# 128 bytes before the weight tiles, and one joint back step per head pair, in a sparse-attention, mixing and MLP kernel

## The chip, the cores and the metric

The kernel runs on one core of one Trainium2 chip. The metric is the device time of one execution in microseconds (us), as the median of several runs. The core has five engines with their own instruction streams: PE (TensorE, matrix products; its weight loads are listed apart as PEld), DVE (VectorE), ACT (ScalarE), POOL (GpSimd) and SP (SyncE, which here only issues DMAs). They wait for one another by semaphores. Matrix products read two operands from SBUF, a stationary one, which a weight load puts into the array, and a moving one, which streams through; they write to PSUM, which has eight banks.

## The reference

```python
def _attn_ref(q, k, v, tau):                 # 4 batches, 8 heads, 576 rows, 64 columns
    scores = 1/sqrt(64) * q @ k.T
    thresh = max(scores, -1) - tau
    attn = exp(where(scores >= thresh, scores, -1e9) - max)
    attn = attn / (sum(attn) + 1e-09)
    return attn @ v
def _moe_ref(x, U, V, w_ch1, w_ch2):         # x: 4 x 576 x 512
    u = x + (x.T @ U @ V).T                  # mixing over the rows, rank 32
    return u + relu(u @ w_ch1) @ w_ch2       # 512 -> 2048 -> 512
def _moe2_ref(x, w_val, conv_w, w_out):
    gate = sigmoid(causal 5-tap convolution of x over the rows, by column)
    return (gate * (x @ w_val)) @ w_out
```

The MLP weights arrive as 64-bit floats and are turned into float32 on the chip. Products of the MLP are made of float32 values split into a high and a low part (`float32r`), with three products for each (high-high, high-low, low-high).

## The kernel before

**Attention.** Two heads form a pair; there are 16 pairs. The 576 rows of a pair's two heads make nine blocks of 128 rows: block 0 holds the last 64 rows of both heads, blocks 1 to 8 alternate between the heads. The main loop runs over *slots* `s`, nine to a pair, one block in each. In slot `s` the engines do this, in the order of the code: `soft_max` of block `s` on DVE (`ns`, L409); then four lists of postponed work, `late[0]` to `late[3]`, filled by `later(slot, list, ...)` and sorted within a list by `LATE_ORDER`; the exponential of block `s` on ACT (`e`, L423) after list 1; the mask and row sum of block `s-1` on DVE (L434) after list 2. Then PE's events of the slot follow, sorted by `ORDER`: the scores of the next block (`s`, L395), the transposes of block `s-2` (`xm`, L451, and for even blocks `xk`, L468), and what the `put` calls assign to the slot.

Counted from a pair's first slot `s0`: the products with V (`pv`, tiles `o`) stand in slots 8 (groups 0 and 1) and 12 (group 2), and their copies to SBUF (`os`, ACT) one slot later. `back` transposes `os` into a PSUM tile `b`, and its results are multiplied by the reciprocal row sums `r` and put into `ring`: for groups 1 and 2 by DVE (L521, 256 columns each), for group 0 by ACT (three small instructions, L534 and L536 twice). `back` of groups 0 and 1 stands in slot 10, of group 2 in slot 14. The row mixing reads `ring`: `mix_t` (`t`, L551) in slot 15, `mix_u` and `mix_ut` in slot 18. A pair's slots 9 to 18 are the next pair's slots 0 to 9. **Below, slots are those of the pair whose scores run**, so `back` stands in slots 1 and 5, `mix_t` in slot 6, `mix_u` and `mix_ut` in slot 0. In slots 0, 1 and 2 `prep_T` transposes q, k and the tails of the pair after it (`tm`, L332 and L335); ACT (L310, L312) and DVE (L316, L320) split them one slot later.

All of `xm`, `xk`, `o`, `b`, `t`, `u`, `ut` and `tm` are PSUM tiles of one pool, `x_ps`, with four banks. A new tile takes the bank that was let go first, so PE waits in the program for the last reader of an older tile. In slot 2 the tile `tm` of the tails (L335) takes the bank of `b`, which both ACT and DVE read; `xm` in slot 3 takes the bank of slot 2's `xm`, or that of `tm` of k.

Between the lists a staged converter (`work.tick`) puts weight conversion steps into the streams of ACT, DVE and POOL (L100 to L128, L167, L169).

**The MLP.** `dense` runs over four chunks `c` of 512 hidden columns and five blocks `n` of rows (four of 512, one of 256). `passes` (L771) makes 48 products per block: `a` with `w1[c % 2]` (stationary) and `us` (moving), `c` with `w2[c % 2]` and `h`. At the end `v` uses `w1[0]` and `us`, and `p` (L917) has a part of `g` as stationary and `w2[0]` as moving operand. Chunks 0 and 2 read `w1_0` and `w2_0`, chunks 1 and 3 `w1_1` and `w2_1`.

Pools lay tiles one behind the other, from the low end of a partition or, with `side="right"`, from the high end. First byte in a partition, before the change:

| tile | placed from | byte | remainder by 512 |
|---|---|---|---|
| `ring` | low | 54112 | 352 |
| `w1_0` | low, behind `ring` | 59232 | 352 |
| `w2_0` | low | 75616 | 352 |
| `w1_1` (pool `big`) | low | 145504 | 96 |
| `w2_1` | high | 163808 | 480 |
| `us`, and the second `us` at the MLP's start | high | 212960, 163808 | 480 |
| `h`, later `g` (two buffers) | high | 180192, 196576 | 480 |

Within these tiles every 128 x 128 weight block and every moving block begins a multiple of 512 bytes further on.

Of the kernel before, what the change touches and what calls it, by code (L numbers as in the profile page):

```python
# [21 lines left out]
F32 = mybir.dt.float32  # L22
# [3 lines left out]
ACTF = mybir.ActivationFunctionType  # L26
ALU = mybir.AluOpType
# [9 lines left out]
def attention_moe_kernel(  # L37
# [15 lines left out]
    nc = tc.nc  # L53
    B, H, S, D = q.shape
# [12 lines left out]
    TL = S - SM  # L67
# [11 lines left out]
    const = ctx.enter_context(tc.tile_pool(name="const", bufs=1))  # L79
    idn = const.tile([128, 128], F32, name="idn")  # L80
# [3 lines left out]
    qscale = const.tile([128, 1], F32, name="qscale")  # L84
    cw = const.tile([128, KC, KD], F32, name="cw")
    u = const.tile([128, KD, T], F32, name="u")
    ring = const.tile([128, 1280], F32, name="ring")
    w1_0 = const.tile([128, 2, KD, FC], F32R, name="w1_0")
    w2_0 = const.tile([128, 2, KD, FC], F32R, name="w2_0")
    wst_p = ctx.enter_context(tc.tile_pool(name="wst", bufs=2))  # L90
# [83 lines left out]
    class Staged:  # L174
# [20 lines left out]
    AT = {  # L195
        "pv": (8, 12), "t": 15, "ut": 18, "u": 18, "Tq": 0, "Tk": 1, "Tt": 2, "stA": 4, "bd": 4, "stB": 5,
        "lq": 1, "lv": 5,
    }
# [24 lines left out]
    def attention(dense_front, dense_mid, dense_back):  # L223
        setup = low.enter_context(tc.tile_pool(name="setup", bufs=1))
        sm_p = low.enter_context(tc.tile_pool(name="sm", bufs=4))
# [23 lines left out]
        st8 = [dict() for _ in range(NP)]  # L249

        def xtile(name):
            return x_ps.tile([128, 512], F32, tag="x", name=name)
# [47 lines left out]
        def later(s, k, fn, name=""):  # L300
            late[k].setdefault(s, []).append((LATE_ORDER.get(name, 0), fn))
# [126 lines left out]
        def row(p, i):  # L428
            return st8[p]["e", i][:, 1 - i % 2 if i else 0, :]

        def soft_mask(p, i):
            d = st8[p]
            e = row(p, i)
            nc.vector.scalar_tensor_tensor(  # L434
                out=e, in0=d.pop(("ns", i)), scalar=d.pop(("th", i))[:, 0:1], in1=e, op0=ALU.is_le, op1=ALU.mult,
                accum_out=d["sum"][:, i:i + 1],
            )
            if i in (4, 8):
                n = slice(0, 5) if i == 4 else slice(5, 9)
                t = d["sum"][:, n]  # L440
                nc.vector.tensor_scalar(out=t, in0=t, scalar1=1e-9, scalar2=None, op0=ALU.add)
                nc.vector.reciprocal(out=d["r"][:, n], in_=t)


        def trans_main(s, p, i):
# [41 lines left out]
        def pv(s, p, *gs):  # L487
            d = st8[p]
            ops = []
            for g in gs:  # L490
                n = 256 if g else TL
                pt = d.pop(("pt", g))
                o = xtile("o")
                nc.tensor.matmul(  # L494
                    o[:, 0:n], vk[p % 2].rearrange("p h d -> p (h d)"), d.pop(("pk", g)), start=True, stop=False
                )
                for j in range(4):
                    for hh in range(2):
                        rhs = pt[:, hh, j, :] if g else pt[:, j, hh * TL:(hh + 1) * TL]
                        ops.append((o[hh * D:(hh + 1) * D, 0:n], vt[p % 2][:, hh, j, :], rhs, j == 3))  # L500
                d["os", g] = os = o_p.tile([128, n], F32, tag=f"os{n}", name="os")
                later(s + 1, 0, lambda os=os, o=o, n=n: nc.scalar.activation(
                    out=os, in_=o[:, 0:n], func=ACTF.Copy), "o")
            for o, lhs, rhs, stop in ops:
                nc.tensor.matmul(o, lhs, rhs, start=False, stop=stop)  # L505


        def back(s, p, *gs):
            x = xtile("b")
            for g in gs:  # L510
                back_group(s, p, g, x)

        def back_group(s, p, g, x):
            d = st8[p]
            os, r = d.pop(("os", g)), d["r"]
            if g:
                for m in range(2):
                    nc.tensor.transpose(x[:, m * 128:(m + 1) * 128], os[:, m * 128:(m + 1) * 128], idn)

                def dve():  # L520
                    nc.vector.tensor_tensor(  # L521
                        out=x_of(p)[:, 2 * g - 2:2 * g, :].rearrange("p t (h d) -> p (t h) d", h=2),
                        in0=x[:, 0:256].rearrange("p (t d) -> p t d", t=4),
                        in1=r[:, 4 * g - 3:4 * g + 1].unsqueeze(2).to_broadcast([128, 4, D]), op=ALU.mult,
                    )

                later(s + 1, 2, dve, "n")
            else:
                x = x[0:TL, 256:384]
                nc.tensor.transpose(x, os[:, 0:TL], idn)  # L530
                rb = sm_p.tile([TL, 1], F32, tag="rb", name="rb")

                def act():
                    nc.scalar.activation(out=rb, in_=r[TL:128, 0:1], func=ACTF.Copy)  # L534
                    for hh, sc in ((0, r[0:TL, 0:1]), (1, rb)):
                        nc.scalar.activation(  # L536
                            out=x_of(p)[0:TL, 4, hh * D:(hh + 1) * D], in_=x[:, hh * D:(hh + 1) * D],
                            func=ACTF.Copy, scale=sc,
                        )

                later(s + 1, 1, act, "nt")

        def x_of(p):
            return ring[:, p % 2 * 640:(p % 2 + 1) * 640].rearrange("p (t d) -> p t d", t=5)
# [39 lines left out]
        for m in range(2):  # L584
# [7 lines left out]
            out=rv[0][:, 0:8 * R].rearrange("p (t r) -> p t r", t=4),  # L592
            in_=moe_U[0:SM, :].rearrange("(t p) r -> p t r", p=128),
# [3 lines left out]
        def load_V(a, o, c, n):  # L597
# [5 lines left out]
            out=qscale, in0=tau_sb, scalar1=0.0, scalar2=float(D) ** -0.5, op0=ALU.is_ge, op1=ALU.mult  # L603
# [39 lines left out]
        def put(s, what, *a):  # L643
            slots[s].append((what, a))

        for p in range(NP):
            s0 = 9 * p
            for i in range(9):
                put(s0 + i + 2, trans_main, p, i)
                if i % 2 == 0:  # L650
                    put(s0 + i + 2, trans_tail, p, i)
            put(s0 + AT["pv"][0], pv, p, 0, 1)
            put(s0 + AT["pv"][0] + 2, back, p, 0, 1)
            put(s0 + AT["pv"][1], pv, p, 2)
            put(s0 + AT["pv"][1] + 2, back, p, 2)
            if p + 1 < NP:
                s1 = s0
                put(s1 + AT["Tq"], prep_T, p + 1, "q")
                put(s1 + AT["Tk"], prep_T, p + 1, "k")
                put(s1 + AT["Tt"], prep_T, p + 1, "tail")  # L660
                put(s1 + AT["stA"], stacks, p + 1, 0)
                put(s1 + AT["bd"], tails, p + 1)
                put(s1 + AT["stB"], stacks, p + 1, 1)
            put(s0 + AT["t"], mix_t, p)
            put(s0 + AT["ut"] - (p == NP - 1), mix_ut, p)
            put(s0 + AT["u"] - (p == NP - 1), mix_u, p)
# [7 lines left out]
        for s in range(NS):  # L674
            p, i = divmod(s, 9)
# [12 lines left out]
            for m in (0, 1, 2, 3):  # L688
                for _, fn in sorted(late[m].pop(s, []), key=lambda x: x[0]):
                    fn()  # L690
                if m == 1 and live:
                    soft_exp(p, i)
                if m == 2 and 1 <= s <= 9 * NP:
                    soft_mask(*divmod(s - 1, 9))
                wtick(m)
# [269 lines left out]
    with tc.manual_schedule():  # L965
        attention(dense_front(), dense_mid, dense_back)
        dense()
# [30 lines left out]
```

## Time and profile before

| | us |
|---|---|
| median of 3 runs (867.21, 868.8, 869.0) | 868.8 |
| the profiled execution, its own time | 867.01 |
| its span in the trace | 865.1 |
| PE busy | 834.6 (96%) |
| DVE busy | 615.9 (71%) |
| ACT busy | 439.9 (51%) |
| POOL busy | 233.4 (27%) |
| `a` and `c` products of the MLP (L771) | 205.6 and 203.0 |

Attention fills the span up to about 345 us, the MLP the rest. The granted clock of TensorE is 1.00 of 2.4 GHz in both stages and 0.87 only between 20 and 60 us. A row of the timeline has the start, the time from there to the end of the last instruction of the group, the engine, line and operation, the tiles (out<-in), the shape and the count; in brackets stands the idle time before it and what ended it. The ends of matrix products are modelled, their starts are recorded.

### The profile page before, as it was taken

Reading aid. Unit: us, or ns where it says so; the run is one execution under the profiler, and the core shown is the slowest. Engines: PE = TensorE matmul, PEld = TensorE weight load, DVE = VectorE, ACT = ScalarE, POOL = GpSimd, SP = SyncE. Lnnn points to the kernel's source line nnn. Section 1 sums busy time; section 2 is a strip of 40 time slices with the busy share of each in tenths; the row PEclk is TensorE's granted clock in tenths of the full one; section 3 lists DMA queues with packets and bytes.
Section 4 is the critical chain, followed back from the end, with each engine's and each line's share of the span. In section 5 each row is a group of like instructions: output and inputs, shape, how many; then the busy total and the mean of one; then the engine's idle time right before and its main releaser. Section 6 shows DMA issues by size and latency. Waiting matters only on the chain.

```text
span 865.1 us, 14250 instructions
## 1 busy us (share of the span) xinstructions
PE 834.6 (96%) x5084; PEld 692.8 (80%) x5084; DVE 615.9 (71%) x1341; ACT 439.9 (51%) x890; POOL 233.4 (27%) x342
## 2 busy tenths in 40 slices
PE   8899999999999999899999999999999999999998
PEld 7687787788787887678888888888888888878886
DVE  5589889889989987436784685357753588988850
ACT  4487888888887887422333333133321334344532
POOL 6645422533322422001331243003420133200000
PEclk9799999999999999999999999999999999999999
DMA  5676755666676651001220122002110111001111
GB/s 129 147 151 124 172 125 125 153 154 137 151 168 135 132 113 44 0 1 49 73 74 25 48 74 74 1 1 84 62 50 1 41 57 49 1 1 49 49 49 74
DMA packets 63423, 68.07 MB, mean 79 GB/s; under 512 B 43333, under 2 KB 46549, under 8 KB 63354
## 3 DMA queue, kind: packets, MB, share of 16 engines
q1 hardware_dynamic: 61786, 64.07, 30.3%
q0 software_dynamic: 1424, 3.10, 1.3%
q8 instruction: 41, 0.67, 0.3%
q14 instruction: 28, 0.23, 0.1%
q10 hardware_dynamic: 144, 0.00, 0.0%
HBM read 35.89 MB, written 4.72 MB: 47 GB/s over the span
## 4 chain that ended last, share of the span: by engine, by line
PE 77%; DVE 9%; ACT 8%; issue 2%; SPq 1%; POOL 1%; DMA 1%; ACTq 0%; DVEq 0%; POOLq 0%
PE a L771 23%; PE c L771 20%; PE o L505 7%; PE s L395 6%; PE p L917 6%; PE xm L451 5%; PE v L771 5%; DVE u L855 3%; ACT e L423 2%; PE t L551 2%; PE o L494 2%; ACT pt L460 2%; DVE ns L409 1%; DVE e L434 1%; ACT qk L310 1%
## 5 line engine op out<-in xcount | busy, mean ns | idle before, releaser
L771 PE MATMUL a<-us,w 128*128 128x512 f32 (+1 forms) x960 | 205.6, 373 | 0.0
L771 PE MATMUL c<-h,w 128*128 128x512 f32 (+1 forms) x960 | 203.0, 370 | 1.3 <-ACT u L573 1.3
L771 PEld LDWEIGHTS a<-us,w 128*128 128x128 f32 x960 | 167.6, 188 | 33.9 <-issue 0.4
L771 PEld LDWEIGHTS c<-h,w 128*128 128x128 f32 x960 | 167.4, 188 | 33.7 <-ACT u L573 1.7
L779 ACT ACTIVATE h<-a 128x512 fp32r<-128x512 f32 (+1 forms) x80 | 44.2, 554 | 202.9 <-PE a L771 202.9
L780 DVE SCALAR_TENSOR_TENSOR h<-a,h 128x512 fp32r<-128x512 f32 (+1 forms) x80 | 51.0, 637 | 112.3 <-ACT h L779 112.2
L423 ACT ACTIVATE e<-ns,nm 128x576 f32<-128x576 f32 x144 | 111.5, 774 | 36.1 <-DVE ns L409 32.7
L128 POOL TENSOR_TENSOR wf<-wf,wt 128x512 f32<-128x512 f32 (+2 forms) x43 | 57.1, 1329 | 262.7 <-DVE wt L123 262.7
L424 POOL TENSOR_TENSOR th<-nm,tau_eff 128x1 f32<-128x1 f32 x144 | 72.8, 506 | 195.5 <-DVE ns L409 193.9
L434 DVE SCALAR_TENSOR_TENSOR e<-ns,th,e 128x576 f32<-128x576 f32 x144 | 119.8, 832 | 5.9 <-POOL th L424 5.5
L409 DVE TENSOR_SCALAR_CACHE_REDUCE ns<-s 128x576 f32<-128x576 f32 x144 | 107.8, 748 | 19.8 <-PE s L395 19.3
L451 PE MATMUL xm<-idn,e 128*128 128x128 f32 x576 | 88.5, 277 | 9.4 <-DVE e L434 5.1
L395 PE MATMUL s<-st 128*128 128x288 f32 x480 | 94.0, 317 | 1.3 <-DVE ns L409 1.1
L460 ACT ACTIVATE pt<-xm 128x512 f32<-128x512 f32 x144 | 84.5, 587 | 2.7 <-PE xm L451 0.6
L451 PEld LDWEIGHTS xm<-idn,e 128*128 128x128 f32 x576 | 69.1, 141 | 15.3 <-ACT pt L460 8.7
L395 PEld LDWEIGHTS s<-st 128*128 128x128 f32 x480 | 68.7, 191 | 13.5 <-DVE ns L409 6.6
L505 PE MATMUL o<-pt,vt 128*64 128x256 f32 (+1 forms) x768 | 70.9, 335 | 0.0
L505 PEld LDWEIGHTS o<-pt,vt 128*64 128x64 f32 x768 | 42.1, 140 | 25.2 <-issue 10.8
L169 POOL TENSOR_TENSOR w<-wf,w 128x512 fp32r<-128x512 f32 x36 | 54.2, 1518 | 10.3 <-ACT w L167 10.3
L832 DVE TENSOR_TENSOR y<-c,y 128x64 f32<-128x64 f32 (+4 forms) x96 | 39.9, 449 | 22.0 <-PE c L771 22.0
L855 DVE SCALAR_TENSOR_TENSOR u<-y,cw,u 128x576 f32<-128x576 f32 x64 | 55.0, 872 | 0.6
L756 DVE TENSOR_TENSOR us<-u,us 128x1024 fp32r<-128x1024 f32 (+1 forms) x40 | 46.8, 1211 | 9.2 <-ACT us L755 9.1
(108 smaller groups left out, 1043.8 us busy)
## 6 DMA issues: line engine op xcount, KB each, us to landing
raw<-in_moe_w_ch_dram SPq DMA_DIRECT2D x32, 512.0 KB, 4.1
st<-qk SPq DMA_DIRECT2D x30, 256.0 KB, 4.1
st<-qk SPq DMA_DIRECT2D x15, 432.0 KB, 4.0
st<-qk SPq DMA_DIRECT2D x45, 144.0 KB, 4.5
out_dram<-ring SPq DMA_DIRECT2D x18, 256.0 KB, 2.0
st<-qk SPq DMA_DIRECT2D x15, 288.0 KB, 4.9
qn<-in_q_dram SPq DMA_DIRECT2D x28, 128.0 KB, 3.8
kn<-in_k_dram SPq DMA_DIRECT2D x28, 128.0 KB, 3.6
```

Source lines behind the costliest of these rows:

```text
L128: nc.gpsimd.tensor_tensor(out=dst, in0=dst, in1=tf, op=ALU.add)
L169: lo_eng.tensor_tensor(out=lo, in0=w, in1=f(hi), op=ALU.subtract)
L395: nc.tensor.matmul(s[:, n, 0:HS], lhs, rhs[:, n * HS:(n + 1) * HS], start=(m == 0), stop=(m == len(ops) - 1))
L409: nc.vector.tensor_scalar(out=ns.rearrange("p (a b) -> p a b", a=2), in0=s, scalar1=-1.0, scalar2=3.0e38, op0=ALU.mult, op1=ALU.min, accum ...
L423: nc.scalar.activation(out=row(p, i), in_=d["ns", i], func=ACTF.Exp, bias=nm[:, 0:1], scale=-1.0)
L424: nc.gpsimd.tensor_tensor(out=th, in0=nm, in1=tau_eff, op=ALU.add)
L434: nc.vector.scalar_tensor_tensor(out=e, in0=d.pop(("ns", i)), scalar=d.pop(("th", i))[:, 0:1], in1=e, op0=ALU.is_le, op1=ALU.mult, accum_o ...
L451: nc.tensor.transpose(x[:, j * 128:(j + 1) * 128], e[:, c + j * 128:c + (j + 1) * 128], idn)
L460: later(s + 1, 0, lambda: nc.scalar.activation(out=dst, in_=x.rearrange("p (j c) -> p j c", j=4), func=ACTF.Copy), "x")
L505: nc.tensor.matmul(o, lhs, rhs, start=False, stop=stop)
L771: nc.tensor.matmul(ps[:, 0:m1], lhs, rhs, start=(m == 0), stop=(m == len(ops) - 1))
L855: nc.vector.scalar_tensor_tensor(out=g, in0=y[:, e, b, k:k + S], scalar=cw[:, k, e:e + 1], in1=g, op0=ALU.mult, op1=ALU.add)
```

## The change

It makes `ring` 32 floats (128 bytes) longer, so everything placed behind it from the low end begins 128 bytes later: `w1_0` at 59360, `w2_0` at 75744, `w1_1` at 145632 (and attention's `u4`, `vt`, `ns`, `e`, `pt`, `os` with them). `ring`, `idn`, `u` and all that is placed from the high end stay. And it joins the three groups' back step: one `back` in slot 14 of a pair with two PSUM tiles (`x0` for group 0, `x` for groups 1 and 2), one DVE multiplication of 512 columns, one sum and one reciprocal of nine columns instead of five and four. ACT's three instructions for group 0 go from list 1 to list 0 of their slot, the `os` copies from list 0 to list 1.

```diff
-    ring = const.tile([128, 1280], F32, name="ring")
+    ring = const.tile([128, 1280 + 32], F32, name="ring")
...
-            if i in (4, 8):
-                n = slice(0, 5) if i == 4 else slice(5, 9)
-                t = d["sum"][:, n]
+            if i == 8:
+                t = d["sum"]
                 nc.vector.tensor_scalar(out=t, in0=t, scalar1=1e-9, scalar2=None, op0=ALU.add)
-                nc.vector.reciprocal(out=d["r"][:, n], in_=t)
+                nc.vector.reciprocal(out=d["r"], in_=t)
...
-                later(s + 1, 0, lambda os=os, o=o, n=n: nc.scalar.activation(
+                later(s + 1, 1, lambda os=os, o=o, n=n: nc.scalar.activation(
                     out=os, in_=o[:, 0:n], func=ACTF.Copy), "o")
...
-        def back(s, p, *gs):
-            x = xtile("b")
-            for g in gs:
-                back_group(s, p, g, x)
-
-        def back_group(s, p, g, x):
+        def back(s, p):
             d = st8[p]
-            os, r = d.pop(("os", g)), d["r"]
-            if g:
-                for m in range(2):
-                    nc.tensor.transpose(x[:, m * 128:(m + 1) * 128], os[:, m * 128:(m + 1) * 128], idn)
-
-                def dve():
-                    nc.vector.tensor_tensor(
-                        out=x_of(p)[:, 2 * g - 2:2 * g, :].rearrange("p t (h d) -> p (t h) d", h=2),
-                        in0=x[:, 0:256].rearrange("p (t d) -> p t d", t=4),
-                        in1=r[:, 4 * g - 3:4 * g + 1].unsqueeze(2).to_broadcast([128, 4, D]), op=ALU.mult,
+            r = d["r"]
+            x0, x = xtile("b0"), xtile("b")
+            for g in (0, 1, 2):
+                os = d.pop(("os", g))
+                if not g:
+                    nc.tensor.transpose(x0[0:TL, 0:128], os[:, 0:TL], idn)
+                    continue
+                for m in range(2 * g - 2, 2 * g):
+                    nc.tensor.transpose(x[:, m * 128:(m + 1) * 128], os[:, m % 2 * 128:(m % 2 + 1) * 128], idn)
+            rb = sm_p.tile([TL, 1], F32, tag="rb", name="rb")
+
+            def act():
+                nc.scalar.activation(out=rb, in_=r[TL:128, 0:1], func=ACTF.Copy)
+                for hh, sc in ((0, r[0:TL, 0:1]), (1, rb)):
+                    nc.scalar.activation(
+                        out=x_of(p)[0:TL, 4, hh * D:(hh + 1) * D], in_=x0[0:TL, hh * D:(hh + 1) * D],
+                        func=ACTF.Copy, scale=sc,
                     )
-                later(s + 1, 2, dve, "n")
...
-                later(s + 1, 1, act, "nt")
+            later(s + 1, 0, act, "nt")
+            later(s + 1, 2, lambda: nc.vector.tensor_tensor(
+                out=x_of(p)[:, 0:4, :].rearrange("p t (h d) -> p (t h) d", h=2),
+                in0=x.rearrange("p (t d) -> p t d", t=8),
+                in1=r[:, 1:9].unsqueeze(2).to_broadcast([128, 8, D]), op=ALU.mult,
+            ), "n")
...
-            put(s0 + AT["pv"][0] + 2, back, p, 0, 1)
             put(s0 + AT["pv"][1], pv, p, 2)
-            put(s0 + AT["pv"][1] + 2, back, p, 2)
+            put(s0 + AT["pv"][1] + 2, back, p)
```

PE, slots 1 and 2 of a pair, before (`s` scores, `xm` and `xk` transposes of `e`, `b` the back transposes, `tm` the preparation of k and of the tails):

```order
L395 MATMUL s<-st 128x288 x4
L451 MATMUL xm<-idn,e 128x128 x4
L468 MATMUL xk<-idn,e 128x128
L530 MATMUL b<-idn,os 64x128
L518 MATMUL b<-idn,os 128x128 x2
L332 MATMUL tm<-idn,kn 128x128 x4
L395 MATMUL s<-st 128x288 x4
L451 MATMUL xm<-idn,e 128x128 x4
L468 MATMUL xk<-idn,e 64x128
L335 MATMUL tm<-idn,tn 128x128
```

The same place now; the three transposes of `b` are gone from it:

```order
L395 MATMUL s<-st 128x288 x4
L450 MATMUL xm<-idn,e 128x128 x4
L467 MATMUL xk<-idn,e 128x128
L332 MATMUL tm<-idn,kn 128x128 x4
L395 MATMUL s<-st 128x288 x4
L450 MATMUL xm<-idn,e 128x128 x4
L467 MATMUL xk<-idn,e 64x128
L335 MATMUL tm<-idn,tn 128x128
```

PE, from the end of slot 5 through slot 6, before, with the engines that each row waits for in the program:

```order
L518 MATMUL b<-idn,os 128x128 [waits Activation_49]
L518 MATMUL b<-idn,os 128x128
L395 MATMUL s<-st 128x288 [waits DVE_49]
L395 MATMUL s<-st 128x288 x3
L451 MATMUL xm<-idn,e 128x128 [waits DVE_49,Activation_49]
L451 MATMUL xm<-idn,e 128x128 x3
L468 MATMUL xk<-idn,e 128x128 [waits Activation_49]
L551 MATMUL t<-ring,u_115 128x128 [waits Activation_49]
L551 MATMUL t<-ring,u_115 128x128
L551 MATMUL t<-ring,u_115 128x128 [waits DVE_49]
L551 MATMUL t<-ring,u_115 128x128 x2
```

The same place now:

```order
L514 MATMUL b_1071<-idn,os 64x128 [waits Activation_49]
L517 MATMUL b<-idn,os 128x128 [waits Activation_49]
L517 MATMUL b<-idn,os 128x128 x3
L395 MATMUL s<-st 128x288 [waits DVE_49]
L395 MATMUL s<-st 128x288 x3
L450 MATMUL xm<-idn,e 128x128 [waits DVE_49,Activation_49]
L450 MATMUL xm<-idn,e 128x128 x3
L467 MATMUL xk<-idn,e 128x128 [waits Activation_49]
L543 MATMUL t<-ring,u_115 128x128 [waits DVE_49,Activation_49]
L543 MATMUL t<-ring,u_115 128x128 x4
```

Five transposes stand where two stood, and the wait for DVE has moved from the third product of `t` to the first. DVE, slots 1 to 3, before:

```order
L409 TENSOR_SCALAR ns,nm<-s 128x576
L434 SCALAR_TENSOR_TENSOR e,sum<-ns,th,e 128x576
L316 SCALAR_TENSOR_TENSOR qk<-tm,qscale,qk 128x512
L409 TENSOR_SCALAR ns,nm<-s 128x576
L521 TENSOR_TENSOR ring<-b,r 128x256
L434 SCALAR_TENSOR_TENSOR e,sum<-ns,th,e 128x576
L320 TENSOR_TENSOR qk<-tm,qk 128x512
```

Now the `ring` row is gone from here (its work is in the 512-column row of slot 6):

```order
L409 TENSOR_SCALAR ns,nm<-s 128x576
L434 SCALAR_TENSOR_TENSOR e,sum<-ns,th,e 128x576
L316 SCALAR_TENSOR_TENSOR qk<-tm,qscale,qk 128x512
L409 TENSOR_SCALAR ns,nm<-s 128x576
L434 SCALAR_TENSOR_TENSOR e,sum<-ns,th,e 128x576
L320 TENSOR_TENSOR qk<-tm,qk 128x512
```

In the four banks, `tm` of the tails now takes the bank of slot 1's `xk`, `xm` of slot 2 that of `tm` of q, and `xm` of slot 3 that of `tm` of k, which DVE reads last (L320). `t` takes the bank of `b` or of `b0`.

## Rows read from the trace of the kernel before

**Rows 1.** The page: the span, and busy time, share and instructions of each engine.

```profile
span 865.1 us, 14250 instructions
PE 834.6 (96%) x5084; PEld 692.8 (80%) x5084; DVE 615.9 (71%) x1341; ACT 439.9 (51%) x890; POOL 233.4 (27%) x342
```

**Rows 2.** Stages: us, busy PE, PEld, DVE, ACT, POOL, granted clock, DMA, GB/s.

```profile
100.00:140.00 40.00, 38.41 (x326) 32.38 (x324) 33.43 (x96) 32.47 (x74) 12.90 (x28) 1.00 0.70 159
...
360.00:865.00 505.00, 496.85 (x2362) 412.34 (x2361) 319.55 (x530) 165.84 (x270) 93.12 (x66) 1.00 0.13 42
```

**Rows 3.** Timeline of PE, blocks of 48 MLP products in chunks 0 to 2.

```profile
440.93 11.36 PE L771 MATMUL c<-h,w 128*128 128x512 f32 x48
...
463.32 5.86 PE L771 MATMUL c<-h,w 128*128 128x256 f32 x48
...
480.16 11.05 PE L771 MATMUL c<-h,w 128*128 128x512 f32 x48
491.05 11.32 PE L771 MATMUL a<-us,w 128*128 128x512 f32 x48
...
562.99 5.91 PE L771 MATMUL c<-h,w 128*128 128x256 f32 x48
...
591.03 11.32 PE L771 MATMUL a<-us,w 128*128 128x512 f32 x48
602.19 11.32 PE L771 MATMUL c<-h,w 128*128 128x512 f32 x48
```

**Rows 4.** Timeline of PE, the last products `v` and `p`.

```profile
782.60 11.30 PE L917 MATMUL p<-w,g 128*128 128x512 f32 x48
793.74 11.35 PE L771 MATMUL v<-us,w 128*128 128x512 f32 x48
```

**Rows 5.** Timeline of PE, slots 1 to 3 of the pair at 164 us.

```profile
165.54 0.27 PE L530 MATMUL b<-idn,os 128*64 128x128 f32 x1
165.65 0.38 PE L518 MATMUL b<-idn,os 128*128 128x128 f32 x2
166.27 0.66 PE L332 MATMUL tm<-idn,kn 128*128 128x128 f32 x4 [0.23 <-DVE qk L316]
...
168.53 0.33 PE L335 MATMUL tm<-idn,tn 128*128 128x128 f32 x1 [0.53 <-DVE ring L521]
...
169.70 0.66 PE L451 MATMUL xm<-idn,e 128*128 128x128 f32 x4 [0.31 <-ACT pt L460]
```

**Rows 6.** Timeline of DVE in the same slots.

```profile
166.13 0.75 DVE L409 TENSOR_SCALAR_CACHE_REDUCE ns<-s 128x576 f32<-128x576 f32 x1
...
168.06 0.42 DVE L521 TENSOR_TENSOR ring<-b,r 128x256 f32<-128x256 f32 x1 [1.17 <-ACT ring L536]
168.40 0.81 DVE L434 SCALAR_TENSOR_TENSOR e<-ns,th,e 128x576 f32<-128x576 f32 x1
...
169.13 0.69 DVE L320 TENSOR_TENSOR qk<-tm,qk 128x512 fp32r<-128x512 f32 x1
```

**Rows 7.** Timeline of ACT in the same slots.

```profile
166.95 0.31 ACT L482 ACTIVATE pk<-xk 128x128 f32<-128x128 f32 x1
...
167.92 0.58 ACT L312 ACTIVATE qk<-tm 128x512 fp32r<-128x512 f32 x1
```

**Rows 8.** Timeline of DVE, slot 2 of the pair at 267 us.

```profile
269.51 0.75 DVE L409 TENSOR_SCALAR_CACHE_REDUCE ns<-s 128x576 f32<-128x576 f32 x1
```

**Rows 9.** Timeline of PE, slot 3 of the pair at 267 us.

```profile
271.63 0.66 PE L451 MATMUL xm<-idn,e 128*128 128x128 f32 x4
```

**Rows 10.** Timeline of DVE, slots 5 and 6 of the pair at 244 us.

```profile
256.88 0.17 DVE L441 TENSOR_SCALAR sum<-sum 128x5 f32<-128x5 f32 x1
257.09 0.19 DVE L442 RECIPROCAL r<-sum 128x5 f32<-128x5 f32 x1
...
257.84 0.42 DVE L521 TENSOR_TENSOR ring<-b,r 128x256 f32<-128x256 f32 x1
```

**Rows 11.** Timeline of PE, the last pair's `t` among the first MLP products.

```profile
367.27 0.94 PE L551 MATMUL t<-ring,u 128*128 128x128 f32 x6 [1.30 <-DVE ring L521]
```

More of the change, by code (lines that the diff above doesn't have):

```diff
@@ L505, in pv @@
                 nc.tensor.matmul(o, lhs, rhs, start=False, stop=stop)
-        def back(s, p, *gs):
-            x = xtile("b")
-            for g in gs:
-                back_group(s, p, g, x)
-        def back_group(s, p, g, x):
-            d = st8[p]
-            os, r = d.pop(("os", g)), d["r"]
-            if g:
-                for m in range(2):
-                    nc.tensor.transpose(x[:, m * 128:(m + 1) * 128], os[:, m * 128:(m + 1) * 128], idn)
-                def dve():
-                    nc.vector.tensor_tensor(
-                        out=x_of(p)[:, 2 * g - 2:2 * g, :].rearrange("p t (h d) -> p (t h) d", h=2),
-                        in0=x[:, 0:256].rearrange("p (t d) -> p t d", t=4),
-                        in1=r[:, 4 * g - 3:4 * g + 1].unsqueeze(2).to_broadcast([128, 4, D]), op=ALU.mult,
-                    )
-                later(s + 1, 2, dve, "n")
[L528 to L539, printed above, removed]
-                later(s + 1, 1, act, "nt")
```

## The prediction

> **What bounds the kernel now.** I read the page first: PE is busy for 834.6 of 865.1 us [rows 1]. The table by stages says that this holds everywhere: 38.41 of 40 us in attention, 496.85 of 505 us in the MLP, both at a granted clock of 1.00, the upper level of 2.4 GHz [rows 2]. So time can come only from two places: from PE's short waits in attention (about 1.6 us in 40), or from PE doing the same products at another pace. Hence the second view, PE's timeline block by block, for the pace; and the third, the timelines of PE, DVE and ACT side by side over the few slots where PE waits.
>
> The pace is not the same everywhere. A block of 48 MLP products of 512 columns takes 11.32 us with `a` (chunk 1 at 491 us, chunk 2 at 591 us) and with `c` in chunk 2, but 11.05 us with `c` in chunk 1 [rows 3]. PE waits for nothing in any of them. The `c` blocks of chunks 1 and 2 differ in one thing, the buffer of their weights: `w2_1` in chunk 1, `w2_0` in chunk 2. The `a` block at 491 us lies right behind a fast `c` block and is slow, so it isn't the stage or what other engines do there.
>
> **128 bytes.** What sets the fast buffer apart is its place against the moving tile. From the table of places: start of the moving operand minus start of the stationary one, remainder by 512, is 0 for `w2_1` with `h` (480 and 480). It is 128 for `w1_0` with `us`, `w2_0` with `h` and `v`, and 384 for `w1_1` with `us` and for `p`. All of these are slow: `a` and `c` above, `p` with 11.30 and `v` with 11.35 us [rows 4]. The place of the weights alone doesn't decide: `p` loads `g` (480, like the fast `w2_1`) as its weights and is slow. After the shift the difference is 0 for `w1_0`, `w2_0`, `v` and `p`, and 256 for `w1_1` (480 - 224).
>
> Terms, as forecast: 16 blocks of `a` and the 8 blocks of `c` with `w2_0`, each 11.32 - 11.05 = 0.27 us: 6.5 us. Four blocks of `v` at 11.35 - 11.05 = 0.30: 1.2 us. 216 products `p`, that is 4.5 blocks, at 0.25: 1.1 us. The 8 `c` blocks with `w2_1` stay. Blocks of 256 columns take 5.86 us with `w2_0` and 5.91 us with `w2_1` [rows 3], so they give nothing. Sum 8.8 us, all on the path, since nothing but PE bounds this stage: DVE is busy 320 of its 505 us [rows 2]. Ends: 0, if the buffer's place has nothing to do with it; 6.6 us, if a difference of 256 is as slow as 128 and 384 (2.2 us less, the 8 `a` blocks of chunks 1 and 3). That 128 and 384 are alike speaks for a period of 256, so I take the whole.
>
> In attention the same shift changes `e` and `os` against `idn` and `u4` against `ring`. The transposes there run at 0.11 us each (from 165.54 to 165.65 [rows 5]), for whatever tile; I put zero, and at most 1 us either way for the 150 products `t`.
>
> **Slots 1 to 3 of a pair.** In the pair at 164 us the chain reads so: DVE's `ring` waits 1.17 us for ACT's part of the same tile [rows 6], `tm` of the tails on PE waits 0.53 us for that, and the next `xm` another 0.31; `tm` of k waits 0.23 [rows 5]. With `back` gone from slot 1 these three waits lose their cause. What is late next? `xm` in slot 3 now needs the bank of `tm` of k, so DVE's L320, and the mask before it. Two chains lead there:
> - DVE: `ns` 166.13 + 0.75, the mask 0.73 (168.40 to 169.13), L320 0.69, some 0.05 to PE: 168.35 [rows 6].
> - ACT: L312 comes right behind `pk`, no longer at 167.92 but at about 167.15 to 167.26, ends 0.58 later, then L320: 168.5 to 168.6 [rows 7].
>
> The later one, 168.5, stands against 169.70 before: 1.2 us earlier. In the pair at 267 us DVE converts weights in slot 1 and comes late to `ns`, 269.51 [rows 8]; the same steps give 271.7 against 271.63 [rows 9], so nothing is gained. These are the ends of 15 pairs; from the same rows of each I get 1.2 us in four, 0.9 in two, 0.2 to 0.6 in seven, 0 in two: 9.5 us together.
>
> PE pays for this in slot 5: three more transposes of 0.11 us [rows 5] in a slot without waits, 0.33 us x 15 = 4.9 us. So the true gain here is only what the waits were, 4.6 us.
>
> **Slots 5 and 6.** DVE loses the sum and the reciprocal (0.17 and 0.19 us [rows 10]) ahead of `ns`, and its `ring` grows from 256 to 512 columns. The trace has no such instruction; its bounds are 0.42 us, the 256-column one [rows 10], and twice that, 0.84; nearest is L320, 512 columns from PSUM, 0.69 us [rows 6], which I take. DVE is then 0.36 - 0.27 = 0.1 us earlier, PE comes 0.33 us later to `t`, but needs the result two products (some 0.4 us) sooner: no change. Queued behind `ring` on DVE is the mask of the block before, which PE needs a slot later; the 0.1 us covers it. ACT's three instructions take 0.66 us (167.26 to 167.92 [rows 7]) and now stand behind slot 6's `pt` and ahead of its exponential; by the same arithmetic they end about when PE reaches `t`. I put 0.1 us a pair, 1.0 us (ends: 0, and 0.3 a pair, 4.5 us). The exponential behind them is needed by DVE only one slot later.
>
> **The last pair** has no scores over it. Its `t` already waits 1.30 us for `ring` between the first two products and the last three [rows 11]. Now all five wait and the instruction is longer: 0.4 + 0.27, a loss of 0.7 us. The `os` copies change lists but not their place among ACT's instructions: zero.
>
> **Sum.** -8.8 - 9.5 + 4.9 + 1.0 + 0.7 = -11.7 us. The profiled execution took 867.0 us, 1.9 us outside its span, so 855.3 us for it. It lies 1.8 us under the median of the three runs, 868.8, and I predict a median: 857.1 us. Own range 853 to 860 (attention between a gain of 7 and none).
>
> **Rivals.**
> 1. *A difference of 256 is slow too.* For it: only 0 is seen fast. Against: 128 and 384 are alike. 857.1 + 2.2 = 859.3 us.
> 2. *The shift does nothing*, and `w2_1` is fast for another reason. For it: one buffer alone is fast, and I infer the rest. Against: every block fits, with stationary and moving exchanged in `p` too. Then 868.8 - 2.9 = 865.9 us. The Trainium skill says so outright (SBUF — State Buffer, "Who interferes with whom"): PE has two independent read ports, one for the moving operand and one for weight loads, and "PE and ACT never wait on anyone". By that rule, two operands' places can't matter. Rows 3 speak against it, with 0.27 us a block; it keeps the chance that one buffer leaves it.
> 3. *Slower: the joint step becomes the wait.* Place: the first product of `t` in slot 6, which now needs DVE's 512 columns and ACT's three instructions. Price: where a converter step of some 0.6 us stands ahead on ACT, 0.6 + 0.6 us, and 15 x 1.2 = 18 us if it were every pair: 857.1 + 17 = 874 us. It decides from about 0.85 us a pair. Against it: the converter works in a few slots only, and PE comes later too.
> 4. *No change:* the shift does nothing and slot 3's new wait for DVE eats the rest: 868 us.
>
> **How the numbers follow.** Forecast 0.55, rival 1 0.20, rival 2 0.13, rival 4 0.07, rival 3 0.05. The time is the forecast's, rounded to 857. The range holds the forecast and rival 1 and goes up to the lower half of rival 2: 852.5 to 865.5. A measurement of this kernel can tell about 0.2% from no change (1.7 us). Faster: 0.55 + 0.20 + 0.13 = 0.88; same 0.07; slower 0.05.
>
> **What would show it.** `a` blocks of chunks 0 and 2, `c` of 0 and 2, `v` and `p` at 11.05 us; `a` of chunks 1 and 3 tell rival 1. PE without the wait for `ring` at L335, and with a wait for DVE's L320 at `xm` in slot 3; `ring` on DVE at 0.69 us without a wait for ACT; slot 5 longer by 0.33 us. The prediction is wrong if these blocks stay at 11.32, or if `t` in slot 6 waits more than 0.3 us in most pairs.

## The result

| | before | after |
|---|---|---|
| median | 868.15 us (4 runs, 867.21 to 869.0) | 859.63 us (4 runs, 858.91 to 860.2) |
| ratio | | 0.9909, 95% interval 0.9889 to 0.9929 |
| profiled execution: time, span | 867.01, 865.1 us | 859.62, 857.6 us |

The changed kernel is faster by 8.5 us; the forecast was 857.0 us with a range of 852.5 to 865.5. Direction and main cause were right, but the single terms don't all agree.

### The profile page after: what moved, and what is told of

The parts are those of the page before. It is cut to its first block, busy times and chain, and to the rows that moved or that the text cites. A ratio compares the mean times of both kernels' runs of the same rounds, so it can differ in the third digit from the quotient of the medians.

```text
span 857.6 us, 14266 instructions
## 1 busy us (share of the span) xinstructions
PE 831.4 (97%) x5084; PEld 698.3 (81%) x5084; DVE 610.0 (71%) x1293; ACT 438.2 (51%) x890; POOL 241.6 (28%) x342
## 4 chain that ended last, share of the span: by engine, by line
PE 79%; DVE 10%; ACT 6%; issue 2%; DMA 2%; POOL 1%; SPq 0%; ACTq 0%; DVEq 0%; POOLq 0%
PE a L762 23%; PE c L762 20%; PE o L504 7%; PE s L395 6%; PE p L908 6%; PE v L762 5%; PE xm L450 5%; DVE u L846 3%; PE t L543 2%; PE o L493 2%; ACT e L423 1%; ACT pt L459 1%; DVE ns L409 1%; DVE qk L320 1%; DVE e L434 1%
## 5 line engine op out<-in xcount | busy, mean ns | idle before, releaser
L762 PE MATMUL a<-us,w 128*128 128x512 f32 (+1 forms) x960 | 203.1, 370 | 0.0
L762 PE MATMUL c<-h,w 128*128 128x512 f32 (+1 forms) x960 | 200.9, 368 | 1.3 <-ACT u L565 1.3
L424 POOL TENSOR_TENSOR th<-nm,tau_eff 128x1 f32<-128x1 f32 x144 | 81.4, 566 | 184.4 <-DVE ns L409 183.6
L762 PE MATMUL v<-us,w 128*128 128x512 f32 (+1 forms) x240 | 52.1, 377 | 2.0 <-DVE us L747 1.1
```

What stands on the lines that cost most here:

```text
L424: nc.gpsimd.tensor_tensor(out=th, in0=nm, in1=tau_eff, op=ALU.add)
L762: nc.tensor.matmul(ps[:, 0:m1], lhs, rhs, start=(m == 0), stop=(m == len(ops) - 1))
```

## The profile after

First the page's parts 1 (span and engines) and the table by stages, which answer [rows 1, 2]:

```profile
span 857.6 us, 14266 instructions
...
PE 831.4 (97%) x5084; PEld 698.3 (81%) x5084; DVE 610.0 (71%) x1293; ACT 438.2 (51%) x890; POOL 241.6 (28%) x342
```

```profile
100.00:140.00 40.00, 38.68 (x328) 32.50 (x327) 34.13 (x93) 32.86 (x78) 14.27 (x28) 1.00 0.70 158
...
365.40:368.90 3.50, 3.50 (x11) 2.82 (x10) 0.00 (x0) 0.00 (x0) 0.00 (x0) 0.51 0.02 5
368.90:372.60 3.70, 3.70 (x17) 3.00 (x16) 0.99 (x2) 0.77 (x2) 0.00 (x0) 1.00 0.00 0
360.00:865.00 505.00, 488.34 (x2348) 411.41 (x2346) 318.89 (x529) 164.95 (x270) 93.01 (x66) 0.99 0.13 42
```

PE is still what bounds both stages. New is the granted clock: 0.51 for 3.5 us behind 365.4 us, where it was 1.00 before.

PE's MLP blocks (timeline), to be set against [rows 3, 4]:

```profile
438.57 11.07 PE L762 MATMUL c<-h,w 128*128 128x512 f32 x48
...
460.36 5.92 PE L762 MATMUL c<-h,w 128*128 128x256 f32 x48
...
477.02 11.04 PE L762 MATMUL c<-h,w 128*128 128x512 f32 x48
487.90 11.04 PE L762 MATMUL a<-us,w 128*128 128x512 f32 x48
...
777.00 11.04 PE L908 MATMUL p<-w,g 128*128 128x512 f32 x48
787.88 11.04 PE L762 MATMUL v<-us,w 128*128 128x512 f32 x48
```

Every block of 512 columns in which PE waits for nothing now takes 11.04 to 11.07 us: those with `w1_0` and `w2_0`, `v`, `p`, and the `a` block at 487.90 with `w1_1` too, whose difference of start is 256. Blocks of 256 columns stay (5.92).

PE in slots 2 and 3 of the pair at 164 us, against [rows 5]:

```profile
163.79 0.60 PE L332 MATMUL tm<-idn,kn 128*128 128x128 f32 x4
...
165.61 0.33 PE L335 MATMUL tm<-idn,tn 128*128 128x128 f32 x1
165.69 0.78 PE L395 MATMUL s<-st 128*128 128x288 f32 x4
166.82 0.66 PE L450 MATMUL xm<-idn,e 128*128 128x128 f32 x4 [0.35 <-DVE qk L320]
```

The waits of both `tm` are gone; what is late next is the one forecast, `xm` for DVE's L320. Slot 6 of the same pair, on PE, ACT and DVE:

```profile
173.43 0.27 PE L467 MATMUL xk<-idn,e 128*128 128x128 f32 x1
173.76 1.38 PE L543 MATMUL t<-ring,u 128*128 128x128 f32 x10
```

```profile
172.34 0.60 ACT L459 ACTIVATE pt<-xm 128x512 f32<-128x512 f32 x1
172.97 0.20 ACT L521 ACTIVATE rb<-r 64x1 f32<-64x1 f32 x1
173.20 0.31 ACT L523 ACTIVATE ring<-b,r 64x64 f32<-64x64 f32 x1
173.41 0.30 ACT L523 ACTIVATE ring<-b,rb 64x64 f32<-64x64 f32 x1
```

```profile
172.69 0.69 DVE L529 TENSOR_TENSOR ring<-b,r 128x512 f32<-128x512 f32 x1
```

Two starts of transposes lie 0.11 us apart [rows 5]; `t` starts 0.33 behind `xk`, 0.05 after ACT's last instruction ends (173.71), and 0.38 after DVE's `ring` (173.38). The list of waits (us in total, times, longest) names ACT as well:

```profile
PEld t L543 <- ACT ring L523: 4.9, 13, 0.7
```

Last, the last pair's `t` and the first two products of the second `v` block, against [rows 11]:

```profile
364.31 1.46 PE L543 MATMUL t<-ring,u 128*128 128x128 f32 x10 [2.01 <-DVE ring L529]
365.45 7.32 PE L762 MATMUL a<-us,w 128*128 128x512 f32 x24
```

```profile
762.97 0.49 PE L762 MATMUL v<-us,w 128*128 128x512 f32 x1 [0.90 <-ACT us L746]
764.59 12.57 PE L762 MATMUL v<-us,w 128*128 128x512 f32 x47 [1.13 <-DVE us L747]
```

24 products in 7.32 us and 47 in 12.57 are 1.6 us too slow each (in the run with filled waits, below, they take 5.74 and 10.96): the clock stood at 0.50, 1.2 GHz, right behind these waits, and the products there started 0.427 us apart.

**Balance.** The slots are measured from the first score product of one to that of the next; pairs 1 to 15.

| term | predicted | span before to after |
|---|---|---|
| pace of the MLP products | -8.8 | -8.6 |
| slots 1 to 3 | -9.5 | -10.4 (117.4 to 107.0) |
| slot 5 | +4.9 | +4.2 (19.5 to 23.7) |
| `t` in slot 6 | +1.0 | +3.8 (35.26 to 39.04) |
| the last pair's `t` | +0.7 | +0.7 (wait 1.30 to 2.01) |
| granted clock behind two waits | none | +3.2 |
| the rest (other slots +0.4, start -0.7, remainder) | none | -0.4 |
| sum | -11.7 | -7.5 |

The first term: from the start of `c` (378.74, now 377.69) to the end 486.4 became 479.9 us, 1.6 of which are given back by the clock, and two `a` blocks lie before it (some 0.5 us).

## Experiments

Slot sums in this section are of pairs 2 to 15, in us. The kernel before took 867.5 to 867.9 us in these comparisons.

| kernel | median us | ratio, interval |
|---|---|---|
| shift alone (e1) | 859.91 | 0.9907, 0.9889 to 0.9924 |
| joint step alone (e2) | 866.47 | 0.9988, 0.9974 to 1.0002 |
| moving side shifted instead (e12) | 858.10 | 0.9902, 0.9881 to 0.9922 |
| 64 bytes (e3) | 861.11 | 0.9927, 0.9911 to 0.9942 |
| 96 bytes (e8) | 868.61 | 1.0006, 0.9995 to 1.0017 |
| `t` a slot later (e4) | 863.26 | 0.9949, 0.9934 to 0.9964 |
| ACT's part ahead of `pt` (e5) | 857.62 | 0.9891, 0.9876 to 0.9907 |
| group 0 a slot earlier (e6) | 857.10 | 0.9885, 0.9871 to 0.9899 |
| group 0 two slots earlier (e9) | 855.73 | 0.9865, 0.9848 to 0.9883 |
| waits filled (e7) | 856.05 | 0.9868, 0.9855 to 0.9881 |
| e9 and filled waits (e10) | 855.36 | 0.9854, 0.9834 to 0.9875 |
| shift alone, filled waits (e11) | 858.47 | 0.9898, 0.9882 to 0.9913 |

**What is each part worth?** The shift alone, and the joint step alone:

```diff
-    ring = const.tile([128, 1280], F32, name="ring")
+    ring = const.tile([128, 1280 + 32], F32, name="ring")
```

> The kernel before with `ring` 32 floats longer, nothing else. Theory (the pace of a product goes by moving start minus stationary start, remainder by 256): all blocks of 512 columns at 11.05 us, those with `w1_1` too; 8.8 us less, some 859.5 us, and the attention slots as before (280.1 us for slots 0 to 8 of pairs 2 to 15). If the fall of the granted clock at the second `v` block (near 765 us in the changed kernel) comes from PE running faster into the same split of `us`, it is seen here as well and gives back some 1.6 us: 861 us. At the last `t` the clock stays at 1.00, since this part of attention is the old one. Rival (the pace gain belongs to the joint step or to both together): no block faster, 868 us.

```diff
-    ring = const.tile([128, 1280 + 32], F32, name="ring")
+    ring = const.tile([128, 1280], F32, name="ring")
```

> The changed kernel with `ring` at its old length: the joint back step alone. Theory: MLP blocks at 11.30 to 11.36 us as before; the slots 1 to 3 of pairs 2 to 15 shorter by 9.4 us, slot 5 longer by 3.9, slot 6 longer by 3.5, so attention gains about 1.6 us, the last pair loses 0.7 us and, if the fall of the granted clock there belongs to the joint step, 1.6 us more: 867.5 to 868.5 us, no difference that can be told from the kernel before. Rival (the joint step is worth the 2.9 us of the prediction): 865 us.

The shift alone brings as much as the whole change (859.91 to 859.63), the joint step alone nothing that can be told (a likely reason stands behind the last experiment). The attention slots behave as in the balance: slots 1 to 3 are 109.5 us with the shift alone and 101.1 with the joint step alone, slot 6 is 33.0 and 36.5. The rows of the joint step alone show the old pace:

```profile
453.15 11.32 PE L762 MATMUL a<-us,w 128*128 128x512 f32 x48
...
481.13 11.05 PE L762 MATMUL c<-h,w 128*128 128x512 f32 x48
```

**Is it the difference of the two starts?** The moving side is shifted instead of the weights:

```diff
+    pad = ctx.enter_context(tc.tile_pool(name="pad", bufs=1, side="right"))
+    pad.tile([128, 32], F32, name="pad")
```

> The kernel before with an unused tile of 128 bytes first at the high end, so that `us`, `h`, `g`, `w2_1` (and attention's `qk` and `st`) begin 128 bytes lower; `ring`, `w1_0`, `w2_0` and `w1_1` stay. By 256 all of `w1_0`, `w2_0`, `w1_1`, `w2_1`, `us`, `h` and `g` then begin at 96; in the changed kernel all begin at 224. Theory (the difference between moving and stationary start decides): all blocks of 512 columns at 226.7 ns a product, 859.9 us as with the shift of the weights. Rival A (the weights' own place decides, 224 by 256 is fast): `a` and `c` stay at 232 to 233 ns, `w2_1` becomes slow too, 870 us. Rival B (both have to be at 224): every block slow, 870 us.

```profile
449.56 11.04 PE L773 MATMUL a<-us,w 128*128 128x512 f32 x48
...
775.46 11.04 PE L919 MATMUL p<-w,g 128*128 128x512 f32 x48
```

All blocks are fast, with weights that haven't moved and all starts at 96 by 256 instead of 224. That leaves the place of the two operands against one another; both rivals fall. Then two other sizes in the kernel before, 16 floats (e3) and in the same line 24 (e8):

```diff
-    ring = const.tile([128, 1280], F32, name="ring")
+    ring = const.tile([128, 1280 + 16], F32, name="ring")
```

> The kernel before with `ring` 16 floats (64 bytes) longer instead of 32. Differences by 512 become 64 for `w1_0`, `w2_0` and `v`, 320 for `w1_1`, 448 for `p`. Theory (only a remainder of 0 by 256 is fast): blocks stay at 11.3 us, 868 us. Rival A (it is enough that the two starts differ by less than 128 bytes by 256): about 859.5 us like the 128-byte shift. Rival B (the penalty falls in steps with the distance): half of it, some 864 us.

> The kernel before with `ring` 24 floats (96 bytes) longer. Differences of start by 256: 32 for `w1_0`, `w2_0`, `v` and `w1_1`, 224 (minus 32) for `p`. With the 64-byte shift (64) products of 512 columns took 228.8 to 229.0 ns and those of 256 columns 113.3, against 226.7 and 119.8 at 0 and 232.4 and 118.6 at 128; `p` at minus 64 stayed at 233.3. Theory A (the pace goes steadily with the difference): 512 columns near 227.7 ns, 256 columns between 113 and 120 ns, `p` between 227 and 233: 860 to 861 us. Theory B (512 columns are as at 0, 256 columns as at 64): 226.7 and 113.3 ns, 3 us less than with 128 bytes, 857 us. Theory C (each difference but 0 costs the same two ns): 860.5 to 861 us with 229 ns.

One `a` block, one of 256 columns and one `p` block with 64 bytes, then an `a` block with 96:

```profile
450.13 11.15 PE L771 MATMUL a<-us,w 128*128 128x512 f32 x48
461.12 5.60 PE L771 MATMUL c<-h,w 128*128 128x256 f32 x48
...
776.72 11.36 PE L917 MATMUL p<-w,g 128*128 128x512 f32 x48
```

```profile
452.33 11.36 PE L771 MATMUL a<-us,w 128*128 128x512 f32 x48
```

With 64 bytes the theory, by which only 0 is fast, and both rivals are wrong: most of the gain is there, blocks of 256 columns are even faster than with 128 bytes (5.60 us instead of 5.92), and `p`, whose operands change roles, is slow. With 96 bytes, between the two, nothing is left; theories A, B and C all fall. So the pace is no steady function of the distance. What rule lies behind it stays open; what is shown is that a remainder of 0 by 256 is good for products of 512 columns, from either side.

**What does `t` wait for in slot 6?**

```diff
-            put(s0 + AT["t"], mix_t, p)
+            put(s0 + AT["t"] + (p < NP - 1), mix_t, p)
```

> The changed kernel with `mix_t` one slot later (slot 7) in all pairs but the last. Theory (ACT's three instructions behind `pt` hold `t` up by some 0.3 us a pair in slot 6): slot 6 goes back by 3.5 us or more (with `t` gone from it), slot 7 grows by the five products of `t` only, so the sum of slots 0 to 8 falls by some 3.5 us and the time to 856 us. Rival (something else becomes late in slots 6 or 7, as the bank of `xm` or the mask, and the wait only changes its name): 859.6 us as the changed kernel.

It is 3.6 us slower than the changed kernel, which neither the theory nor the rival had. Slots 6 and 7 together lose 1.9 us (49.1 to 47.2), but slot 8 grows by 6.3: `o` of the products with V takes the bank of `t`, and DVE's subtraction that reads it (L545) is now late.

```profile
PEld o L493 <- DVE t_st L545: 6.3, 11, 0.9
```

```diff
-        "T": 1, "n": -1, "nt": -2, "o": -1, "t": 2, "u": 1, "x": -2,
+        "T": 1, "n": -1, "nt": -3, "o": -1, "t": 2, "u": 1, "x": -2,
```

> The changed kernel with ACT's three instructions for group 0 ahead of `pt` in list 0 of their slot instead of behind it. Theory (in slot 6, `t` waits for the end of ACT's group 0 part, 0.33 us a pair, and DVE's `ring` ends 0.33 us earlier): slot 6 of pairs 2 to 15 falls from 36.5 to some 33 us; `pt` comes 0.7 us later, and if nothing waits for its bank in slots 7 and 8 the time is 856 us. Rival (the wait passes to the `xm` that needs the bank which `pt` lets go, or to the exponential and the mask): slots 6 to 8 together as in the changed kernel, 107.9 us, and 859.6 us.

For the next, `back` keeps groups 1 and 2, and a new `back0` has the transpose of group 0 and ACT's three instructions:

```diff
+            put(s0 + AT["pv"][1] + 1, back0, p)
             put(s0 + AT["pv"][1] + 2, back, p)
```

> The changed kernel with the back step of group 0 (its transpose and ACT's three instructions) one slot earlier, that of groups 1 and 2 where it is. Theory as for the run with ACT's part first: the wait of `t` for ACT goes, 3.5 us in slot 6, and no `pt` comes later in slot 6, so 856 us. Rival (the two extra places in the order make the exponential of slot 5 late by 0.7 us, and its mask and transposes follow): slot 7 or 8 grows by as much and it is 859 to 860 us.

In neither did slot 6 fall (36.6 and 36.3, against 36.5), so the theory, that `t` waits for the data of ACT's group 0, is wrong. The lists of waits of the two:

```profile
PEld t L543 <- ACT pt L459: 4.0, 13, 0.4
```

```profile
PEld t L546 <- ACT pt L459: 3.4, 11, 0.6
```

The two medians lie 2.0 and 2.5 us under the changed kernel's, but not by their slots: slots 0 to 8 sum to 278.4 and 278.3 us, against 278.5. The granted clock is the likely cause; its mean is on record for every run. In e6 the time goes with it: 856.2 and 856.3 us at 0.992, 857.1 at 0.990, 858.5 and 859.0 at 0.988. The changed kernel's four runs stood at 0.987 to 0.990, but don't line up so among themselves, so this isn't shown.

`t` now waits for `pt`, which has no part in its data. It has one in its bank: in the changed kernel the program gives `t` the bank of `b0` in 13 of 15 pairs (last read by ACT's group 0 part) and that of `b` in two; in these two kernels, in the same 13 pairs, that of slot 5's `xm` (last read by `pt`). In the changed kernel exactly those 13 pairs have a longer slot 6, by 0.3 to 0.4 us (2.20 to 2.53 in most); the two others are shorter by 0.25 and 0.29. ACT has hardly a gap in slots 5 and 6, so 0.66 us more there come before whatever frees that bank. So group 0 was moved to where ACT idles, slot 4:

```diff
+            put(s0 + AT["pv"][1], back0, p)
             put(s0 + AT["pv"][1] + 2, back, p)
```

> The changed kernel with the back step of group 0 two slots earlier: its transpose in slot 3, ACT's three instructions in slot 4, where ACT idles 0.76 us before the copy `os`. In the two runs before, `t` in slot 6 waited as long as in the changed kernel, now by ACT's `pt` (the bank that `t` takes was read by it), in the same 13 of 15 pairs. Theory (what counts is that ACT has 0.66 us more to do just ahead of `pt` in slots 5 and 6, in whatever order; the waiting name follows the bank): with this work in ACT's gap of slot 4, slot 6 falls from 36.5 to some 33 us over pairs 2 to 15, slot 5 by 1.5 us, slot 3 grows by 1.5 us; the sum of the slots falls from 278.4 to some 275 us, the time to 854 to 856 us. Rival (ACT's gap in slot 4 isn't free, since the copy `os` and the exponential behind it then come late): slot 4 or 5 grows by 3 us, 857 to 859 us.

The wait for ACT is gone from the list, slots 5 and 6 lose 3.1 us, slot 3 gains 2.5; the sum falls by 0.8 us only (278.5 to 277.7). So of the 3.9 us by which the median lies under the changed kernel's the slots give 0.8; for the rest the granted clock is again the likely cause: three of e9's four runs had a mean of 0.992, as the two fastest of e6. Slot 6 is 2.37 us in most pairs, half-way. PE, ACT and DVE there:

```profile
174.13 1.35 PE L546 MATMUL t<-ring,u 128*128 128x128 f32 x10
```

```profile
172.95 0.60 ACT L459 ACTIVATE pt<-xm 128x512 f32<-128x512 f32 x1
```

```profile
173.29 0.69 DVE L532 TENSOR_TENSOR ring<-b,r 128x512 f32<-128x512 f32 x1
```

ACT is done at 173.55, DVE's `ring` ends at 173.98, and `t` starts at 174.13: behind ACT's wait stood DVE's, 0.17 us a pair, from the longer joint multiplication. The list of waits names DVE for a few of them only and puts most down to "issue":

```profile
PEld t L546 <- issue: 2.9, 11, 0.8
```

But in 14 of the 15 pairs the first weight load of `t` starts 0.115 or 0.116 us after the end of DVE's `ring`, while the time since ACT's `pt` goes from 0.20 to 0.84 us. The first two products once needed only what slot 2 had made.

**The granted clock.** 16 transposes of `idn` into the tile that follows, ahead of the last `t` and of the second `v` block:

```diff
+            for _ in range(16 if p == NP - 1 else 0):
+                nc.tensor.transpose(x, idn, idn)
...
+                for _ in range(16 if n == 1 and e == 0 else 0):
+                    nc.tensor.transpose(ps[:, 0:128], idn, idn)
```

> The changed kernel with 16 transposes of `idn` without use put on PE ahead of the last pair's `t` and 16 ahead of the second `v` block, where PE waits 2.01 and 0.90 + 1.13 us. Theory (the granted clock falls to 0.50 there, for 3.41 us each time, because PE has been waiting just before): the clock stays at 1.00 at both places, the first `a` block and this `v` block have all products at 227 ns, and 1.6 us a place come back, up to 3.3 us in the profiled execution and 1 to 3 us in the median, with less spread between the runs: 857 to 858.5 us. Rival (the fall has nothing to do with the wait): the clock falls at the same places, 859.6 us.

```profile
362.49 1.91 PE L543 MATMUL t<-idn 128*128 128x128 f32 x16
364.66 1.38 PE L545 MATMUL t<-ring,u 128*128 128x128 f32 x10 [0.26 <-DVE ring L529]
365.79 5.74 PE L764 MATMUL a<-us,w 128*128 128x512 f32 x24
...
763.33 10.96 PE L764 MATMUL v<-us,w 128*128 128x512 f32 x47 [0.54 <-DVE us L749]
```

Both stretches run at full pace and the median is 3.6 us under the changed kernel's, with intervals that don't touch. But the wait is not all of it. With the same 2.01 us ahead of `t`, the run with `t` a slot later kept 1.00, as did that with group 0 two slots earlier; the one with 64 bytes kept it behind 0.92 and 1.13 us at `v`. Of the eleven profiled executions with these waits open (before and after among them), six show a fall at one place or both, and the three with filled waits show none. At `t` it is three of the six with a wait of 2.01 us, and none of the five with the old 1.30. The runs that weren't profiled fit this: the mean granted clock of all four runs of e7 is 0.991 to 0.994. That a wait of PE can be followed by such a fall, and that none came where the waits were filled, are facts of these runs; what decides in which execution it comes stays open. The Trainium skill (TensorE: Matmul & The Clock Gate, "What's actually happening") calls what a slow clock costs at a kernel's start "run-variable" for one and the same kernel. The falls in the middle vary here in the same way: e5's five runs, on one chip, took 857.0 to 857.6 us at a mean granted clock of 0.990 and 859.9 and 860.2 us at 0.988.

Both remedies together, and the shift alone with filled waits (10 and 16 transposes):

> The run with group 0 in slot 3 and the 16 + 16 transposes without use in PE's two waits, together. Theory (both gains are separate): 3.4 us under the run with the filled waits (856.05 us), 852.5 to 853 us, with the clock at 1.00 from 40 us to the end. Rival (only one of them counts): 855 to 856 us.

> The kernel before with 32 floats more in `ring` and 10 transposes without use ahead of the last pair's `t` (its wait there is 1.30 us) and 16 ahead of the second `v` block: the shift alone with the granted clock held up, to be set against the changed kernel with the same (856.05 us). Theory (the joint step is worth 2 to 2.5 us over the pairs and loses 0.7 us in the last): 857.3 to 858 us. Rival A (the joint step is worth nothing): 856 us. Rival B (it is worth the 2.9 us of the prediction): 859 us.

The first, 855.36 us, is the fastest measured, but can't be told from e7 or e9: it lies 0.7 us under e7, about what its slots gave (0.8), not 3.4. The theory had counted e9's whole gain as its slots', and the rival came out. The second sizes the joint step with the clock held up: 858.47 us with the shift alone, 856.05 with the whole change (e7), some 2.4 us, with intervals that don't touch; the prediction's own terms for it come to 2.9. Without the filling the clock is likely to have met most of this gain: in the profiled executions of the changed kernel and of e2 it falls twice, in those of e1 and of the kernel before once and never.

## Why the prediction was right, and where not

- **128 bytes.** Right in cause and size (-8.6 for -8.8), and for the stated reason: e12 shows that it is the place of the two operands against one another, not that of the weights, which makes these blocks slow or fast. The chosen end, that 256 is as good as 0, held. The inference from 128 and 384 being alike to a period of 256 came out for 0 and 256, but it was no rule for the rest: 32 and 64 behave unlike what any smooth rule would give. Rival 1 (859.3 us) lies close to the measured median for another reason; the `a` blocks with `w1_1` refute it.
- **Rival 2** falls: the shift alone makes 8 us. The sentence of the Trainium skill that stood for it (SBUF — State Buffer, "Who interferes with whom"), that PE's two read ports are independent and PE waits on nobody, doesn't cover what is measured: products that wait for no engine take 232 to 233.4 or 226.7 ns by the places of their two operands.
- **Slots 1 to 3.** Right, with the order of what is late next: in the pair at 164 us DVE's L320 starts 0.16 us late behind ACT's L312, and `xm` behind L320. The pair at 267 us, where no gain was counted, gained none (7.68 us before, 7.66 after).
- **Slot 5**: 0.28 us a pair for 0.33; the cost was laid where it is.
- **`t` in slot 6** is the term that was mis-sized: 0.1 us a pair was put, 0.25 measured, 3.8 us for 1.0, inside the end of 4.5. The failed step is the arithmetic by which ACT's three instructions "end about when PE reaches `t`". In the pair at 164 us PE could have started `t` 0.11 us behind `xk`, at 173.54, and ACT ends at 173.71. The data of group 0 is needed by the fifth product only; PE waits for the bank, and so at the first. DVE's side failed too: "no change" was 0.17 us a pair, hidden behind ACT's wait.
- **The last pair** lost the 0.7 us foreseen. What came behind the longer wait, the clock at half, was not foreseen; with the fall at `v`, which the shift alone shows too, it is 3.2 us in the profiled execution.
- **The total.** On the span, `t` and the clock cost 6.0 us more than put, and small gains elsewhere met 1.8 of them. The median, 2.6 us over the forecast, is off by less, because the profiled execution before lay under its median and the one after lies on it; that is luck. With the clock held up the changed kernel takes 856.05 us, 1 us from the 857.1 worked out, but there too the loss at `t` is partly met by gains that were not put.

## What to carry to other kernels

Before tuning waits on a PE-bound kernel, compare the time of equal blocks of products by buffer: where they differ, line up the starts of the stationary and the moving operand (here: equal by 256 bytes), from whichever side is easier to move. When a step is moved, follow the rotating PSUM banks as well as the data, because the next tile may wait for whoever last read the bank. A wait of PE can cost more than its length, since the products behind it may run at half clock; work without use in it is free if it ends before the data comes.

## What the runs showed of the hardware

| moving start minus stationary start, by 256 | 512 columns, ns a product | 256 columns |
|---|---|---|
| 0 | 226.6 to 227.5 | 119.6 to 119.9 |
| 32 | 233.3 | 116.7 to 117.8 |
| 64 | 228.8 to 229.3 | 113.3 to 117.8 |
| 128 | 232 to 233.4 | 118.5 to 120.1 |
| 192 and 224 (`p` in e3, e8) | 233.3 | |

These are means over blocks of 48 products, start to start. One `v` block between two `p` blocks in e3 took 233.3 at 64, so the pace also depends on something else, which was not found. In six of eleven executions the granted clock stood at half for a while (0.51 over 3.5 us in the row of the stages) behind 1.7 to 2.0 us of waiting in one or two pieces, and products of 512 columns then took 427 ns.
